# Retention heads in (batch, row) order: keys and values used as they were loaded

## The chip, the cores and the metric

The kernel runs on one core of one Trainium2 chip. The metric is the device time of one execution in microseconds, lower is better. Two figures appear below: the time of an execution, and the span of the profiled execution, from its first to its last instruction, which is a little shorter.

## The reference

Retention (attention with a decay instead of a softmax) on 8 batches, 8 heads, 576 positions and 64 dimensions, then a two-layer network with a hard-swish gate on the 4608 tokens of 512 values that come out.

```python
scores = scale * np.matmul(q, k.transpose(0, 1, 3, 2))
gamma = 1.0 - 2.0 ** (-5.0 - np.arange(H, dtype=np.float32))
rel = pos[:, None] - pos[None, :]
Dmat = np.where(rel >= 0, gamma[:, None, None] ** rel[None, :, :], 0.0)
attn = np.matmul(scores * Dmat[None, :, :, :], v)
x = np.ascontiguousarray(attn.transpose(0, 2, 1, 3)).reshape(B * S, H * D)
h = x @ w_in
out = (h * np.clip(h + 3.0, 0.0, 6.0) / 6.0) @ w_out
```

## The kernel before

**Blocks.** The 576 positions of a batch are cut into the first 64 (TL), here called the head block, and 512 more in four chunks of 128. Block 0 of the kernel (`kb` 0) holds the head blocks of all eight batches, 512 tokens; blocks 1 to 8 hold the other 512 positions of one batch each. In blocks 1 to 8 the positions before a chunk reach it through a running state per head, which begins with the state that the head block leaves. So block 0 has to give two things: its own outputs (`xts[0]`, the transposed input of the network), and for each batch and head a 64 by 64 state, the decayed product of keys and values (`zh`).

**Block 0 before the change.** Heads are taken in four pairs (`i` = 0 to 3, NP). `load_half` (line 415) and `load_values` (460) load one head of a pair for all batches: 128 partitions, each with four adjacent positions (`j`, NJ = 4) of 64 values, 1 KB. Position `4 r + j` of batch `b` lies in partition `8 r + b`. q and the first k are loaded in float32 by SP and ScalarE and cast by VectorE (`cast_heads`, 435); the other k and all v are loaded and cast to fp16 by DMAs that GpSimd issues. `turn_heads` (440) transposes k and q with TensorE; its moving operand `by_chunk` (84, 104) is a permuted identity that sorts the columns by batch, so that after the copy out of PSUM two batches stand side by side in each of four groups of 128 columns (`c`, NCB). `scores_heads` (492) then has one product of 128 by 128 for each group and head, and a masking product on VectorE with `hmask` (115, 152), 128 by 128 per head, which holds the decay and zero between the two batches of a group. The values are still in the order of the load: `values_heads` (470) sorts them with 32 products against `pick` (454, 456). The keys for the state are turned back by `keys_heads` (478) and scaled by their decay in `scaled_heads` (484). `inner_heads` (505) multiplies masked scores and sorted values, `head_states` (281) makes the states, `heads_decayed` (295) moves them to `zh`.

**After it.** `up_steps` (523) makes one unit of the up product of a block: four pairs of products (`product`, 154, two 64-column halves), a ScalarE pass (545) and a VectorE pass (547). Block 0 has 16 units; the first four are started in turn, interleaved. `fetch(8, wout[0])` (874) holds back SP's loads of the chunks until the first piece of w_out has landed. Later stages overlap the retention of block `kb + 1`, the up product of the next and the down product of the last block.

**Order.** The order on every engine is written out by hand (from line 794): each engine works through its instructions in program order, and a wait stops what is queued behind it. PSUM has two rings of buffers: `st` with two and `pp` with six, given out in turn, so a new tile waits until its buffer's last reader is done. GpSimd computes and also issues DMAs: first k and v, then four pieces of w_in (715), then four of w_out (723). DMAs of GpSimd share eight semaphores in turn, so a DMA is issued when the one eight places ahead has landed.

The diff touches these functions:

## Time and profile before

| what | value |
|---|---|
| median of 3 runs | 293.78 us (293.6 to 297.28) |
| profiled execution, its own time | 294.78 us |
| its span | 292.9 us |
| TensorE busy | 284.6 us, 97% |
| VectorE, ScalarE, GpSimd busy | 73%, 63%, 46% |
| granted TensorE clock | 1.00 |
| HBM read, written | 36.70 MB, 9.44 MB |

The profile names an instruction by the line of the kernel that wrote it and by its tiles, output first: `L502 ha<-hpa,ws` is line 502, writing `ha16` from the scores in PSUM and the mask, which lies in a tile of `ws`. PE is a product on TensorE, PEld its weight load, DVE is VectorE, ACT ScalarE, POOL GpSimd, SP the engine that issues most DMAs; a `q` behind the name means the engine's sequencer. Behind "idle before" stands how long the engine had waited and for whom. DMA queues: q1 is SP's, q10 ScalarE's, q0 GpSimd's. [...]

### The profile page before, as it was taken

Reading aid. Unit: us, or ns where it says so; the run is one execution under the profiler, and the core shown is the slowest. Engines: PE = TensorE matmul, PEld = TensorE weight load, DVE = VectorE, ACT = ScalarE, POOL = GpSimd, SP = SyncE. Lnnn points to the kernel's source line nnn. Section 1 sums busy time; section 2 is a strip of 40 time slices with the busy share of each in tenths; the row PEclk is TensorE's granted clock in tenths of the full one; section 3 lists DMA queues with packets and bytes.
Section 4 is the critical chain, followed back from the end, with each engine's and each line's share of the span. In section 5 each row is a group of like instructions: output and inputs, shape, how many; then the busy total and the mean of one; then the engine's idle time right before and its main releaser. Section 6 shows DMA issues by size and latency. Waiting matters only on the chain.

```text
span 292.9 us, 12624 instructions
## 1 busy us (share of the span) xinstructions
PE 284.6 (97%) x5574; PEld 222.4 (76%) x5574; DVE 214.8 (73%) x380; ACT 185.4 (63%) x326; POOL 133.8 (46%) x166
## 2 busy tenths in 40 slices
PE   7899999999999999999999999999999999999995
PEld 2776556887656589787778788878788977778894
DVE  7858948888866867789776978697868685747654
ACT  4968546856775877647675768476847574655420
POOL 8961148788651527066625662656265004000510
PEclk9999999999999999999999999999999999999999
DMA  7999999999999999979998999798916101200114
GB/s 161 166 204 214 238 233 219 244 226 226 208 167 199 187 238 197 190 202 215 281 183 202 174 235 143 191 180 221 124 69 102 51 4 65 83 0 2 74 74 143
DMA packets 119526, 47.86 MB, mean 163 GB/s; under 512 B 92336, under 2 KB 114864, under 8 KB 119472
## 3 DMA queue, kind: packets, MB, share of 16 engines
q1 hardware_dynamic: 114336, 41.56, 73.1%
q0 software_dynamic: 4704, 5.11, 10.7%
q8 instruction: 43, 0.70, 1.1%
q10 hardware_dynamic: 432, 0.39, 0.5%
q14 instruction: 11, 0.09, 0.1%
HBM read 36.70 MB, written 9.44 MB: 158 GB/s over the span
## 4 chain that ended last, share of the span: by engine, by line
PE 94%; DMA 2%; ACT 1%; issue 1%; DVE 0%; SPq 0%; DVEq 0%
PE ph L158 44%; PE pm L158 29%; PE pd L158 10%; PE po L241 4%; PE pa L241 2%; DMA hq<-in_q_dram 2%; PE pu L241 2%; PE hpv L158 1%; PE ptk L158 1%; PE ptq L158 1%; ACT hqT L449 1%; ACT hkT L451 0%; PE hpo L511 0%; PE hptq L444 0%; SPq L424 0%
## 5 line engine op out<-in xcount | busy, mean ns | idle before, releaser
L158 PE MATMUL ph<-xT,win 128*64 128x512 f16 (+1 forms) x1248 | 145.6, 364 | 0.3 <-issue 0.3
L547 DVE SCALAR_TENSOR_TENSOR g<-u,ph 128x512 f16<-128x512 f32 x132 | 89.6, 684 | 51.5 <-ACT u L545 51.2
L545 ACT ACTIVATE u<-ph,half 128x512 f32<-128x512 f32 x132 | 90.2, 690 | 42.4 <-PE ph L158 41.5
L158 PEld LDWEIGHTS <-win 128*64 128x64 f16 x1248 | 85.2, 136 | 26.1 <-issue 0.9
L158 PEld LDWEIGHTS <-g 128*64 128x64 f16 x928 | 53.3, 110 | 16.5 <-issue 0.7
L158 PEld LDWEIGHTS <-s 128*64 128x64 f16 x896 | 51.1, 110 | 8.1 <-issue 0.7
L158 PE MATMUL pm<-ws,s 128*64 128x256 f16 x672 | 46.1, 273 | 0.5 <-issue 0.5
L333 POOL TENSOR_TENSOR z<-z,gpow 128x256 f32<-128x256 f32 x24 | 15.5, 644 | 65.6 <-DVE z L332 47.7
L199 POOL TENSOR_TENSOR q<-fq,dec 128x512 f16<-128x512 f32 x31 | 35.7, 1171 | 8.5 <-DMA fq<-in_q_dram 8.5
L394 ACT CAST xT<-po 128x512 f16<-128x512 f32 (+1 forms) x36 | 21.8, 676 | 24.3 <-PE po L241 24.3
L651 POOL TENSOR_TENSOR u<-u,p 128x512 f32<-128x512 f32 x7 | 8.9, 1270 | 61.4 <-ACT u L692 55.2
L204 POOL TENSOR_TENSOR v<-fv,dec 128x512 f16<-128x512 f32 x32 | 35.6, 1113 | 0.1
L158 PE MATMUL pm<-wout,g 128*64 128x256 f16 x448 | 32.2, 273 | 0.0
L158 PE MATMUL pd<-wout,g 128*64 128x512 f16 x256 | 31.9, 380 | 0.3 <-issue 0.3
L276 DVE TENSOR_TENSOR a<-pa,mask 128x512 f16<-128x512 f32 (+1 forms) x36 | 21.0, 625 | 4.7 <-PE po L241 2.7
L587 DVE TENSOR_TENSOR s<-g 128x1024 f16<-128x1024 f16 x28 | 19.4, 695 | 0.2
L193 ACT CAST k<-fk 128x512 f16<-128x512 f32 x24 | 14.9, 621 | 4.0 <-DMA fk<-in_k_dram 4.0
L342 ACT CAST z<-z 128x512 f16<-128x512 f32 x24 | 14.9, 622 | 4.0 <-DVE z L329 4.0
L158 PE MATMUL pm<-ws,g 128*64 128x256 f16 x224 | 16.8, 274 | 0.0
L158 PE MATMUL pm<-wout,s 128*64 128x256 f16 x224 | 16.6, 273 | 0.0
L587 DVE TENSOR_TENSOR s<-g,s 128x1024 f16<-128x1024 f16 x14 | 12.1, 862 | 0.0
L241 PE MATMUL po<-qT,z 64*64 64x64 f16 x512 | 10.9, 196 | 0.3
(112 smaller groups left out, 280.8 us busy)
## 6 DMA issues: line engine op xcount, KB each, us to landing
fk<-in_k_dram SPq DMA_DIRECT2D x32, 256.0 KB, 4.6
fq<-in_q_dram SPq DMA_DIRECT2D x16, 512.0 KB, 5.9
fv<-in_v_dram SPq DMA_DIRECT2D x32, 256.0 KB, 5.8
out_dram<-o SPq DMA_DIRECT2D x14, 512.0 KB, 4.0
win<-in_moe_w_in_dram POOLq DMA_DIRECT2D x4, 512.0 KB, 9.0
wout<-in_moe_w_out_dram POOLq DMA_DIRECT2D x4, 512.0 KB, 17.1
out_dram<-o SPq DMA_DIRECT2D x7, 256.0 KB, 5.0
hq<-in_q_dram SPq DMA_DIRECT2D x6, 128.0 KB, 4.7
```

What stands on the lines that cost most here:

```text
L158: nc.tensor.matmul(out[r], lhs[:, r], rhs, skip_group_check=True, **flags)
L193: cast_keys = lambda: (nc.gpsimd.tensor_copy if c in K_POOL else nc.scalar.copy)(by_head(k16), in_rows(st[c]["fk"]))
L199: (nc.vector if e and c in Q_DVE else nc.gpsimd).tensor_tensor(by_head(q16[:, e]), in_rows(st[c]["fq"][:, :, e, :]), in_rows(dd[:, 2 + e, ...
L204: nc.gpsimd.tensor_tensor(v16, st[c]["fv"], dd[:, 1, H:2 * H, :], ALU.mult)
L241: return lambda: nc.tensor.matmul(*args, skip_group_check=True, **flags)
L276: nc.vector.tensor_tensor(a16[:, a, 0:n].rearrange("p x i q -> p (x i) q"), pa[a].rearrange("p x i q -> p (x i) q"), m, ALU.mult)
L333: nc.gpsimd.tensor_tensor(new, new, decay, ALU.mult)
L342: nc.scalar.copy(z16s[c], zs[c])
L394: nc.scalar.copy(xt[:, s], po[s].rearrange("p x n (e r) -> p x n e r", e=2))
L545: nc.scalar.activation(uu[:, 0:n], ph[:, 0:n], ACTF.Relu, bias=half, scale=1.0 / 6.0)
L547: nc.vector.scalar_tensor_tensor(out=g[:, hf, ths, jr, :], in0=by_half(uu), scalar=1.0, in1=by_half(ph), op0=ALU.min, op1=ALU.mult)
L587: nc.vector.tensor_tensor(*pend.popleft())
```

## The change

Loads put position `4 r + j` of batch `b` into partition `16 b + r`: the source is walked batch by batch instead of row by row. 32 partitions then hold two batches, and scores, inner and state products are made for each group of 32 partitions (`rows32`) and each `j`, with keys and values as they were loaded. q is still sorted by the copy that follows its turn. The score products grow from 8 to 32 for a pair of heads, the inner products from 8 to 32, the state products from 64 to 128 in all. The sorts (`values_heads`), the second turn of the keys (`keys_heads`, `scaled_heads`), `by_chunk`, `picks` and the clearing of `pick` go. The mask of a head has 134 columns instead of 128, and the four `j` read it at four shifted places. The decay of the keys moves to the values: `values_apart` writes, for each pair, the values of the even and of the odd batch of a group apart, with decay and zeros, on GpSimd for pairs 1 and 3 and on VectorE for 0 and 2. Inner products of all pairs gather in four PSUM tiles (`po`), copied out in eight pieces (`outputs_heads`). In the order, all masks and the exponents of k stand ahead of the turns of q, GpSimd's w_out DMAs stand behind its two `values_apart`, and 16 idle products stand ahead of the first up products. Cut to its core:

```diff
-        nc.gpsimd.iota(query, pattern=[[TL, 2], [1, NJ], [NJ, RP]], base=0, channel_multiplier=0,
+        nc.gpsimd.iota(query, pattern=[[P, 2], [1, NX]], base=1 - NJ, channel_multiplier=0,
                        allow_small_or_imprecise_dtypes=True)
...
-        nc.vector.tensor_copy(by_chunk.rearrange("p (c e r) -> p c e r", c=NCB, e=2),
-                              ident16.rearrange("p (r e c) -> p c e r", e=2, c=NCB))
...
+        if of == "k":
+            nc.vector.tensor_copy(fk[:, 0:1], fj[:, 0:1])
+            for e in range(2):
+                nc.vector.scalar_tensor_tensor(out=base[:, e:e + 1], in0=odd, scalar=(2 * e - 1) * FAR, in1=row,
+                                               op0=ALU.mult, op1=ALU.add)
+            nc.vector.tensor_scalar(base[:, 1:2], base[:, 1:2], 1.0, -FAR, ALU.mult, ALU.add)
+            nc.vector.tensor_tensor(fk[:, 1:].rearrange("p (e j) -> p e j", e=2), steps,
+                                    base.unsqueeze(2).to_broadcast([P, 2, NJ]), ALU.add)
...
-                nc.vector.tensor_scalar(arg[:, :, H + h], fj[:, 0:4], -lg, 0.0, ALU.mult, ALU.add)
+                nc.vector.tensor_scalar(argk[:, :, h], fk, -lg, 0.0, ALU.mult, ALU.add)
...
-    hmask = ws[3].rearrange("p j n -> p (j n)")[:, 0:H * P].rearrange("p (h q) -> p h q", h=H)
+    hmask = ws[3].rearrange("p j n -> p (j n)")[:, 0:H * 2 * NX].rearrange("p (h x) -> p h x", h=H)
...
-    def head_states(c0, tag):
...
+    def head_states(pu, i):
+        for j in range(NJ):
+            for t in range(NCB):
+                at = rows32(t)
                 for a in range(2):
-                    j, h2 = divmod(i + NP * a, 2)
-                    for e in range(2):
-                        todo[e].append(mm(pu[e][rows(a), c - c0, i], kn[rows(e), j, c, h2 * D:h2 * D + D],
-                                          vh[rows(e), c, j, h2, :], start=True, stop=True))
-        in_turn(todo)
-        return pu
-
-    def heads_decayed(c0, e, pu):
-        z, by = zh[:, c0 + NCB * e:c0 + NCB * e + 2], gpow.unsqueeze(1).unsqueeze(3).to_broadcast([P, 2, NP, D])
-        if e:
-            nc.scalar.copy(z, pu[e])
+                    n, h2 = divmod(i + NP * a, 2)
+                    nc.tensor.matmul(pu[t][rows(a), i], hd[n]["k"][at, h2, j, :], vh[n][at, h2, :, j, :],
+                                     start=(j == 0), stop=(j == NJ - 1), skip_group_check=True)
+
+    def heads_decayed(t, pu, on_dve):
+        z, by = zh[:, 2 * t:2 * t + 2], gpow.unsqueeze(1).unsqueeze(3).to_broadcast([P, 2, NP, D])
+        of = pu[t].rearrange("p i e d -> p e i d")
+        if on_dve:
+            nc.vector.tensor_tensor(z, of, by, ALU.mult)
+        else:
+            nc.scalar.copy(z, of)
             nc.gpsimd.tensor_tensor(z, z, by, ALU.mult)
...
-    def idle_products(n):
+    def idle_products(n, of=NP):
...
-    kn = ws[1].rearrange("p j n -> p (j n)").rearrange("p (i c x) -> p i c x", i=NP, c=NCB)
-    vh = ws[4].rearrange("p j n -> p (j n)").rearrange("p (c i e d) -> p c i e d", c=NCB, i=NP, e=2)
+    rows32 = lambda t: slice(2 * RP * t, 2 * RP * t + 2 * RP)
+    vh = [ws[1 + i // 2].rearrange("p j n -> p (j n)")[:, (i % 2) * 4 * NJ * D:(i % 2 + 1) * 4 * NJ * D].rearrange(
+        "p (h e j d) -> p h e j d", h=2, e=2, j=NJ) for i in range(NP)]
 
...
-                            dict(q=q, k=k, v=v)[nm][:, 2 * i + e, 0:TL, :].rearrange("b (r j) d -> r b (j d)", j=NJ))
+                            dict(q=q, k=k, v=v)[nm][:, 2 * i + e, 0:TL, :].rearrange("b (r j) d -> b r (j d)", j=NJ))
...
-                nc.tensor.matmul(pt[e * D:e * D + D, j, :], hd[i][nm][:, e, j, :], by_chunk, start=True, stop=True,
+                nc.tensor.matmul(pt[e * D:e * D + D, j, :], hd[i][nm][:, e, j, :], ident16, start=True, stop=True,
                                  skip_group_check=True)
...
+            t = half_tile(work, "qT", i, FP16, "hqT", bufs=3)
+            copy(t.rearrange("p (x r j) -> p x r j", j=NJ, r=RP), pt.rearrange("p j (x r) -> p x r j", r=RP))
+            hd[i]["qT"] = t.rearrange("p (t y) -> p t y", t=NCB)
...
-    def picks():
...
+            t = work.tile([P, H * D], FP16, tag="kT", bufs=4, name=f"hkT{i}").rearrange("p (j x) -> p j x", j=NJ)
+            copy(t, pt)
+            hd[i]["kT"] = t
...
-                                    v[:, 2 * i + e, 0:TL, :].rearrange("b (r j) d -> r b (j d)", j=NJ))
+                                    v[:, 2 * i + e, 0:TL, :].rearrange("b (r j) d -> b r (j d)", j=NJ))
...
-    def values_heads(i, copy):
...
-    def keys_heads(i, tag):
...
-    def scaled_heads(i, on_dve):
...
+    def values_apart(i, engine):
+        by = deck[:, 1:, 2 * i:2 * i + 2].rearrange("p (e j) h -> p h e j", e=2)
+        for h2 in range(2):
+            engine.tensor_tensor(vh[i][:, h2], hd[i]["v"][:, h2].unsqueeze(1).to_broadcast([P, 2, NJ, D]),
+                                 by[:, h2].unsqueeze(3).to_broadcast([P, 2, NJ, D]), ALU.mult)
 
     def scores_heads(i):
         kT, qT = hd[i]["kT"], hd[i]["qT"]
-        a16 = work.tile([P, 2, NCB, P], FP16, tag="a16", bufs=4, name=f"ha16_{i}")
-        pa = [psum.tile([P, NCB, P], FP32, tag="pp", name=f"hpa{h2}_{i}") for h2 in range(2)]
-        for c in range(NCB):
-            for h2 in range(2):
-                r = slice(h2 * D, h2 * D + D)
-                nc.tensor.matmul(pa[h2][:, c, :], kT[r, c, :], qT[r, c, :], start=True, stop=True)
+        a16 = work.tile([P, 2, NJ, P], FP16, tag="a16", bufs=4, name=f"ha16_{i}")
+        pa = [psum.tile([P, NJ, P], FP32, tag="pp", name=f"hpa{h2}_{i}") for h2 in range(2)]
+        for j in range(NJ):
+            for t in range(NCB):
+                for h2 in range(2):
+                    nc.tensor.matmul(pa[h2][rows32(t), NJ - 1 - j, :], kT[rows(h2), j, rows32(t)], qT[rows(h2), t, :],
+                                     start=True, stop=True, skip_group_check=True)
         for h2 in range(2):
-            m = hmask[:, 2 * i + h2:2 * i + h2 + 1, :].to_broadcast([P, NCB, P])
-            nc.vector.tensor_tensor(a16[:, h2], pa[h2], m, ALU.mult)
+            m = hmask[:, 2 * i + h2, :]
+            m = bass.AP(m.tensor, m.offset, [list(m.ap[0]), [1, NJ], [NX, 2], [1, TL]])
+            by_half = lambda t: t.rearrange("p j (e s) -> p j e s", e=2)
+            nc.vector.tensor_tensor(by_half(a16[:, h2]), by_half(pa[h2]), m, ALU.mult)
         hd[i]["a16"] = a16
 
-    def inner_heads(i, copy):
+    def inner_heads(i):
         if 0 not in xts:
             xts[0] = work.tile([P, NP, BLK], FP16, tag="xT", bufs=2, name="xT0")
-        po = psum.tile([P, NCB, P], FP32, tag="pp", name=f"hpo{i}")
-        for c in range(NCB):
-            for h2 in range(2):
-                nc.tensor.matmul(po[h2 * D:h2 * D + D, c, :], vh[:, c, i, h2, :], hd[i]["a16"][:, h2, c, :],
-                                 start=True, stop=True, skip_group_check=True)
-        copy(xts[0][:, i, :].rearrange("p (x r j) -> p x r j", r=RP, j=NJ),
-             po.rearrange("p c (e j r) -> p (c e) r j", e=2, j=NJ))
+            hd["po"] = [psum.tile([P, NP, P], FP32, tag="st" if t < 2 else "pp", name=f"hpo{t}",
+                                  **(dict(bufs=2) if t < 2 else {})) for t in range(NCB)]
+        for j in range(NJ):
+            for t in range(NCB):
+                at = rows32(t)
+                for h2 in range(2):
+                    nc.tensor.matmul(hd["po"][t][rows(h2), i, :], hd[i]["v"][at, h2, j, :], hd[i]["a16"][at, h2, NJ - 1 - j, :],
+                                     start=(j == 0), stop=(j == NJ - 1), skip_group_check=True)
+
+    by_pairs = lambda: xts[0].rearrange("p n x -> p (n x)").rearrange("p (g t i x) -> p g t i x", g=2, t=NCB, i=2)
+
+    def outputs_heads(g, t, copy):
+        copy(by_pairs()[:, g, t], hd["po"][t][:, 2 * g:2 * g + 2, :])
...
+        if kb == 0:
+            to, x = ph.rearrange("p (t x) -> p t x", t=NCB), lambda dmc: by_pairs()[:, dmc // 2, :, dmc % 2, :]
...
-                nc.gpsimd.memset(pick.rearrange("p j c m -> p (j c m)").bitcast(I32), 0)
+                nc.gpsimd.iota(steps, pattern=[[0, 2], [1, NJ]], base=0, channel_multiplier=0,
+                               allow_small_or_imprecise_dtypes=True)
         for i in range(NP):
             load_values(i)
         for n in range(4):
             win_piece(n)
-        wout = [wout_piece(pc) for pc in (0, 2, 1)]
-        decays_of_chunk()
-        wout.append(wout_piece(3))
-        decays("q")
-        mask_of_chunk()
         distances()
         idle_products(8)
-        mask_of_heads(0)
+        for i in range(3):
+            mask_of_heads(i)
         cast_heads(0, "k", on_dve)
-        picks()
         decays("k")
         turn_heads(0, "k", on_act)
-        mask_of_heads(1)
+        mask_of_heads(3)
+        exponents("k")
         idle_products(3)
         cast_heads(0, "q", on_dve)
-        mask_of_heads(2)
         turn_heads(0, "q", on_act)
         cast_heads(1, "q", on_dve)
         turn_heads(1, "k", on_act)
         turn_heads(1, "q", on_act)
         cast_heads(2, "q", on_dve)
         scores_heads(0)
-        mask_of_heads(3)
-        exponents("k")
-        keys_heads(0, "pp")
         turn_heads(2, "k", on_act)
         turn_heads(2, "q", on_act)
         cast_heads(3, "q", on_dve)
         scores_heads(1)
-        keys_heads(1, "pp")
         turn_heads(3, "k", on_act)
         turn_heads(3, "q", on_act)
         scores_heads(2)
-        scaled_heads(0, False)
-        values_heads(0, on_act)
+        inner_heads(0)
         scores_heads(3)
-        scaled_heads(1, False)
-        values_heads(1, on_act)
-        inner_heads(0, on_act)
-        values_heads(2, on_dve)
-        inner_heads(1, on_dve)
-        values_heads(3, on_act)
-        inner_heads(2, on_dve)
-        keys_heads(2, "st")
-        scaled_heads(2, True)
+        inner_heads(1)
+        for t in range(NCB):
+            outputs_heads(0, t, on_act)
+        for i in (1, 3):
+            values_apart(i, nc.gpsimd)
+        wout = [wout_piece(pc) for pc in (0, 2, 1)]
+        decays_of_chunk()
+        wout.append(wout_piece(3))
+        decays("q")
+        mask_of_chunk()
+        inner_heads(2)
+        values_apart(0, nc.vector)
+        inner_heads(3)
+        idle_products(16, 1)
+        for t in range(NCB):
+            outputs_heads(1, t, on_act if t % 2 else on_dve)
+        values_apart(2, nc.vector)
         first = [up_steps(0, u) for u in range(4)]
-        for unit in first:
-            next(unit)
-        inner_heads(3, on_act)
-        keys_heads(3, "st")
-        scaled_heads(3, False)
-        for unit in first:
-            next(unit)
+        for _ in range(2):
+            for unit in first:
+                next(unit)
         for unit in first:
             for _ in unit:
                 pass
-        heads = [head_states(0, "pp"), head_states(2, "st")]
+        pu = [psum.tile([P, NP, 2, D], FP32, tag="st" if t < 2 else "pp", name=f"hpu{t}",
+                        **(dict(bufs=2) if t < 2 else {})) for t in range(NCB)]
+        for i in range(NP):
+            head_states(pu, i)
         fetch(8, wout[0])
-        heads_decayed(0, 0, heads[0])
         for u in range(4, NFC):
             up_unit(0, u)
             if u == 4:
-                heads_decayed(0, 1, heads[0])
+                heads_decayed(2, pu, True)
+            elif u == 5:
+                heads_decayed(3, pu, False)
             elif u == 9:
-                heads_decayed(2, 0, heads[1])
+                heads_decayed(0, pu, True)
             elif u == 10:
-                heads_decayed(2, 1, heads[1])
+                heads_decayed(1, pu, False)
             elif u == 12:
                 exponents("q")
         weight_sums(3, 1, 2, 4)
```

## The prediction

> **What bounds the kernel now.** I read the page first. TensorE is busy for nearly all of the span, so the change can only matter where TensorE isn't yet full, or by what it makes TensorE wait for later.

> ```profile
> PE 284.6 (97%) x5574; PEld 222.4 (76%) x5574; DVE 214.8 (73%) x380; ACT 185.4 (63%) x326; POOL 133.8 (46%) x166
> ```

> So I went to the chain in order of time for the start of the span. Its columns are start, length, and what the chain runs through.

> ```profile
> 1.57 5.63 DMA hq<-in_q_dram
> ...
> 16.18 0.89 PE hpv L158 x32
> 17.08 0.22 PE hpo L511 x8
> 17.30 0.22 PE hpk L158 x8
> ...
> 21.66 0.67 PE pu L241 x64
> 22.33 10.51 PE ph L158 x96
> ```

> From 22.33 on TensorE runs up products without a gap (96 in 10.51 us, 0.1095 us each), and what follows is untouched. The change is worth what it does to that one time stamp, plus any later wait that it makes. Before it lie the q load, the turns, and, until 17.1, the sorting of values on TensorE (`hpv`). The timeline of VectorE shows what runs beside that.

> ```profile
> 9.83 1.29 DVE L502 TENSOR_TENSOR ha<-hpa,ws 128x512 f16<-128x512 f32 x2 [0.47 <-PE hpa L499]
> 11.04 0.42 DVE L437 CAST hq<-hq 128x512 f16<-128x512 f32 x1
> 11.37 3.85 DVE L502 TENSOR_TENSOR ha<-hpa,ws 128x512 f16<-128x512 f32 x6
> ```

> VectorE masks scores until 15.22 with no gap after the last cast of q (0.64 us a mask): the masks follow that cast by queue order, and the cast needs the last q load. The third view is the DMA of the first 14.2 us.

> ```profile
> DMA  0000004899869899999999999999999999897936
> ...
> q0 software_dynamic: 2078, 0.98, 59.2%
> q1 hardware_dynamic: 1008, 0.92, 23.0%
> q10 hardware_dynamic: 432, 0.39, 10.3%
> ```

> After six empty slices (2.1 us) the engines are full: 92.5% of 14.2 us of sixteen engines. The packets also tell how a load is spread: q10 carries three loads of 128 rows, 384 packets, and has 432; q1 seven loads, 896, and has 1008. Each load brings 16 short packets more. Every load of today has a source whose outermost loop counts 16 (`r b (j d)`) or a multiple of it.

> **Part one, what is taken off TensorE.** The four value sorts are 128 products of 0.0278 us (0.89 us for 32), 3.6 us on the chain; the four key turns 4 x 0.22 = 0.9 us. The sorting copies behind them go from ScalarE and VectorE, such as

> ```profile
> L476 ACT CAST ws<-hpv 128x512 f16<-128x512 f32 x3 | 1.8, 585 | 1.2 <-PE hpv L158 1.2
> ```

> Of these 4.5 us little comes back: the masks end at 15.22 either way, and the last inner product, the up products and the states stand behind them.

> **Part two, what is added before the up products.** The masks keep their size (six after the cast, 3.85 us). Behind them VectorE now has two products of `values_apart(0)`, 512 elements each, then two of the four copies of `outputs_heads(1, t)`, 256 elements out of PSUM. The first is nearest to a half of q16 on VectorE, the second to a state sum:

> ```profile
> L199 DVE TENSOR_TENSOR q<-fq,dec 128x512 f16<-128x512 f32 x1 | 0.7, 693 | 1.7 <-DMA fq<-in_q_dram 1.7
> ...
> L329 DVE TENSOR_TENSOR z<-pa,zh 128x256 f32<-128x256 f32 x1 | 0.4, 425 | 0.6 <-PE pa L241 0.6
> ```

> That is 1.38 + 0.85 us. The copies make a new wait: the four first up units take PSUM buffers in turn, and the second and third take those of `po` 2 and 3, so only the first product pairs of unit 0 can run before both copies of `po` 2 are done. Everything on TensorE queues behind that wait, and ScalarE and VectorE wait for its `ph`. ScalarE's share of the copies ends earlier, since it has only waited for the same inner product.

> After it come 32 up products less one pair, 3.50 - 0.22 = 3.28 us, then the states: 128 products of 32 rows and 128 columns instead of 64 of 64 and 64. 32-row tiles stand nowhere in the trace. Today's 64 take 0.67 us, 10.5 ns each; two at a time, as in the sort, would take 13.9, so more than two run at once. Low end: eight at a time, 128 x 27.8 / 4 = 0.89 us. High end: two at a time, 3.56 us. I take the rate of the nearest row, 10.5 ns, 1.34 us. Scores and inner products (32 for 8 per pair of heads, each) cost 0.34 us for 0.22 by it, beside the masks, which take 1.28 us a pair; without that cover they would add 0.1 us a pair.

> If the loads land as now, the cast starts at 11.04 and the sum is 11.04 + 0.42 + 3.85 + 1.38 + 0.85 + 0.1 (handovers) + 3.28 + 1.34 = 22.26: nothing gained (22.33).

> The rest of the front is covered.

> ```profile
> L118 ACT ACTIVATE ws<-early,scale 128x128 f16<-128x128 f32 x8 | 2.7, 394 | 1.3 <-DVE early L113 1.3
> ```

> These masks of ScalarE now all stand ahead of the q turns, with the exponents of k, from 4.9 to 8.2, where ScalarE waits for q (the cast of q came at 7.3); uncovered they would add 0.7 us. `decays("k")` gains five tiny steps where VectorE waits for q as well. Up products read `xT` in pieces of 128 columns, still 512 a product. GpSimd gets four products of 512 elements at 1.11 us, 4.5 us ahead of the four w_out DMAs, the powers, `decays("q")` and the chunk mask. Behind w_out wait SP's loads:

> ```profile
> L199 POOL TENSOR_TENSOR q<-fq,dec 128x512 f16<-128x512 f32 x6 | 6.6, 1113 | 8.5 <-DMA fq<-in_q_dram 8.5
> ```

> ```profile
> 14.55 1.64 POOL L724 DMA_DIRECT2D wout<-in_moe_w_out_dram x3
> ```

> ```profile
> SPq L179 <- DMA wout<-in_moe_w_out_dram: 22.3, 1, 22.3
> ```

> ```profile
> L719 POOL DMA_DIRECT2D win<-in_moe_w_in_dram x4: 760/765/797, 11.6 to 13.8; - x4
> ...
> DMA to landing us min/median/max: 5.9/9.0/12.6
> ```

> The last w_in piece, issued at 13.8, lands 12.6 us later, at 26.4. The DMA engines limit that stream, so w_out issued at 19 instead of 14.6 still finds w_in in front of it: covered as long as it is issued before some 26.

> **Part three, the loads.** All 24 head loads keep their bytes and 128 rows of 1 KB, but the source now reads `b r (j d)`: the outermost loop counts 8. What this costs isn't in the trace. Bounds: nothing, if the rows are dealt out as before; and twice the engines' time for these loads, if a load is shared out along that loop, as the 16 closing packets beside an outer 16 suggest, so that eight engines carry it. I take the second, as the nearest reading of the packets.

> [...]

> The price, from rows. The last q load is issued at 5.8 and lands some 4.7 us on, at 10.5:

> ```profile
> L424 SPq DMA_DIRECT2D hq<-in_q_dram x6: 536/599/797, 1.6 to 5.8; - x6
> ...
> DMA to landing us min/median/max: 4.3/4.7/5.6
> ```

> Hardware loads (q1 and q10) are 33.3% of 14.2 us, 4.73 us on each of sixteen engines; software head loads 59.2%, less some first w_in packets, 8.2 us. Between 2 and 11 us the engines work off 110%, 1.10 us per us:

> ```profile
> q0 software_dynamic: 1413, 0.65, 57.9%
> q1 hardware_dynamic: 1008, 0.92, 36.3%
> q10 hardware_dynamic: 432, 0.39, 16.2%
> ```

> With 8 of the 14 software loads (4.7 us) served beside them, the last q load would land at 2.1 + (4.73 + 4.7) / 1.10 = 10.7: the model holds for today. On eight engines the hardware part is 9.46 us. With 8 of 14 software loads beside it: 2.1 + 14.2 / 1.10 = 15.0; with all of them: 2.1 + 17.7 / 1.10 = 18.2. I take 15.8, near the low end, since the last software loads are issued late. The cast then starts at 15.8 instead of 11.04, with masks of three pairs still behind it, and the up products run free at 22.26 + 4.76 = 27.0, that is 4.7 us later than now. The weights are delayed by about as much (the eight engines hold 17.7 us of head loads instead of 12.9), so SP's loads stay in step with TensorE.

> **The sum.** The profiled execution took 294.78 us for its span of 292.9, which is 1.0 above the median of 293.78.

> ```profile
> span 292.9 us, 12624 instructions
> ```

> 294.78 + 4.7 = 299.5 on its scale; on that of the median 298.5.

> **The rivals.** First, not slower: the loads land as now, because rows are dealt out over sixteen engines whatever the outer loop. For it: nothing in the trace shows a load on fewer. Against: the closing packets. The sum above then gives 22.26, or 293.7 us; with states at either end 293.2 to 295.9. It decides if the last q load lands by 11.0.

> Second, TensorE works at half rate, or its 32-row products take turns. The first idle products show a half rate:

> ```profile
> 1.85 3.63 PE L158 MATMUL idle<-ident 128*64 128x512 f16 x16 [1.85 <-POOL ident masks.py:199]
> ```

> 0.227 us each against 0.1095. With q late, TensorE has little to do from 7.2 to some 20. Up products of units 0 to 3 at half rate cost 3.3 us more, states two at a time 2.2: 300.7 to 301.8 with late loads. Against: the sixteen idle products put ahead of them, and gaps of one or two us only.

> [...]

> Third, w_out comes too late. With v landing at 18, GpSimd would issue w_out near 21. If w_in has run dry by then, the loads of chunk 4 slip; now q16 starts only just before its turn:

> ```profile
> 39.34 1.46 POOL L199 TENSOR_TENSOR q<-fq,dec 128x512 f16<-128x512 f32 x1 [8.49 <-DMA fq<-in_q_dram]
> ...
> 41.31 0.66 PEld L158 LDWEIGHTS <-q 128*64 128x64 f16 x16
> ```

> That leaves 0.5 us; 3 us of slip beyond TensorE's own would give 301. Against: w_in would then end near 30.

> **How the numbers follow.** Forecast 0.60 (298.5; 297 to 301 by its bounds), not slower 0.22 (293.7), half rate or serial products 0.13 (301), w_out 0.05 (301). The 2% that a measurement of this kernel can tell from no change is 5.9 us: 299.7 and 287.9. Slower by that: a quarter of the forecast's case (0.16), nearly all of the second rival (0.12), most of the third (0.04): 0.32. Faster by that: no case reaches it, 0.02 for what I don't see; within it 0.66. The range takes in the rival of the other side and the upper bounds: 293.0 to 302.0.

> **What would show it.** Right: hq's landings stretch from 4.7 to 8 us and more, the last cast of q on VectorE starts near 15.8, q10 has 408 packets for its three loads (8 closing ones each), and the run of 96 up products starts near 27, with masks, two products and two copies back to back ahead of it on VectorE. Wrong: the cast at 11 with 432 packets (first rival); states over 2 us, or up products of units 0 to 3 at 0.2 us each (second); TensorE's `ptq` later behind the 96 up products than now (third).

## The result and the profile after

The changed kernel is slower: 304.33 us (median of 4 runs, 302.35 to 305.37) against 294.2 for the kernel before beside it, a ratio of 1.0314 with an interval of 1.0222 to 1.0406. The profiled execution took 304.93 us for a span of 303.1. The forecast of 298.5 and its range up to 302.0 lie below.

The chain in order of time (start, length, what it runs through) again gives the time stamp that the prediction is about:

```profile
6.76 7.78 DMA hk<-in_k_dram
...
18.61 1.88 PE hpo L502 x50
20.50 0.67 PE idle L167 x9
21.17 1.25 issue
22.42 1.49 PE idle L167 x23
23.91 5.25 PE ph L167 x32
29.15 1.22 PE hpu L296 x128
30.38 10.51 PE ph L167 x96
```

The 96 up products start at 30.38 instead of 22.33, 8.05 us late, and themselves take 10.51 us as before. The remaining 2.1 us or so of the span are lost later. Three things in these rows have no counterpart before: a pause in which TensorE waits for nothing that the profile shows ("issue"), 32 up products at 0.164 us each (5.25 us over 32) where 0.1095 were forecast, and, behind the pause, idle products that were to fill a gap and now come after it. Such rates are the length of a group over its count, since the products overlap: the page has 0.367 us as the mean of one product of `ph`, and 146.3 us as busy time of all 1248. VectorE's timeline has the fourth:

```profile
14.44 0.43 DVE L443 CAST hq<-hq 128x512 f16<-128x512 f32 x1 [0.72 <-DMA hq<-in_q_dram]
...
18.93 4.65 DVE L474 TENSOR_TENSOR ws<-hv,deck 128x512 f16<-128x512 f16 x2
23.50 0.74 DVE L508 CAST xT<-hpo 128x256 f16<-128x256 f32 x2
24.17 1.28 DVE L474 TENSOR_TENSOR ws<-hv,deck 128x512 f16<-128x512 f16 x2
```

The two products of `values_apart(0)` take 4.65 us; the same two for pair 2 take 1.28 at 24.17. What differs is GpSimd, which makes its own four products of line 474 in the same time (4.6 us by the groups of instructions).

The windows view gives the granted clock (the number behind POOL's):

```profile
10.00:15.00 5.00, 3.80 (x100) 2.60 (x99) 2.61 (x6) 2.35 (x5) 2.61 (x5) 0.53 1.10 161
15.00:20.00 5.00, 4.56 (x195) 3.09 (x193) 4.63 (x7) 2.27 (x6) 5.00 (x7) 0.50 0.89 117
...
26.00:28.00 2.00, 2.00 (x15) 1.35 (x13) 0.00 (x0) 0.10 (x1) 1.68 (x10) 0.65 1.26 214
```

TensorE runs at half clock from soon after 10 us to 27.4 (0.65 over the last window is a half for 1.4 of its 2 us), though it counts as busy for 4.56 of the 5 us from 15 to 20, with the new small products. The kernel before has 1.00 from 7.58 us to its end. The stretch just ahead of the drop shows TensorE waiting for the casts of late q loads, busy for 1.09 of 3.41 us:

```profile
6.93:10.34 3.41, 1.09 (x18) 0.55 (x16) 0.63 (x2) 1.13 (x4) 2.76 (x5) 1.00 1.07 200
```

The pause is read from windows that all begin at zero: the numbers behind the first two busy times are TensorE's products and weight loads so far.

```profile
0.00:22.00 22.00, 15.59 (x351) 9.04 (x351) 13.64 (x43) 10.27 (x25) 16.57 (x31) 0.74 0.85 141
0.00:90.00 90.00, 82.14 (x1757) 56.17 (x1758) 67.71 (x133) 52.29 (x101) 58.46 (x94) 0.91 1.05 195
...
0.00:156.00 156.00, 146.44 (x3035) 106.00 (x3036) 116.89 (x212) 96.61 (x177) 88.93 (x123) 0.95 1.07 199
```

Each window ends inside a pause (from 21.17, 89.24 and 155.54). The sums are 702, 3515 and 6071 instructions: 11 and 21 times 256 above the first, within 7 (some records can be missing). Counted the same way, every pause of TensorE over 0.12 us behind its first 20 instructions that has no releaser, in all fourteen traces of this case, stands within some 15 of such a multiple. So in these traces TensorE makes such stops only where a block of 256 instructions ends. The queue that carries instructions (q8) fits:

```profile
q0 software_dynamic: 6496, 5.12, 10.8%
q8 instruction: 44, 0.72, 1.0%
q10 hardware_dynamic: 408, 0.39, 0.4%
```

44 packets of 16 KB for 11,404 products and weight loads (2 x 5702), one for every 259. The first packet behind a block's edge at 17.0 starts at 20.16, and TensorE goes on 2.26 us after that. The kernel before has the same edge, ahead of its states, at 21.65, and does not stop there: its packet started at 18.17. In both kernels the packet starts about 3 us after TensorE passed the block's edge ahead of it (17.0 here, 15.35 before) and takes 0.9; the difference is how soon the block at hand is used up, in 4.2 us here and in 6.3 before. What starts a packet, no trace shows. Single pauses of this kind last up to 3.79 us in the runs here (`before_split_sort`, 16.87 to 20.66).

### The profile page after: what moved, and what is told of

Read it like the earlier page. It is cut to its first block, busy times and chain, and to the rows that moved or that the text cites. A ratio compares the mean times of both kernels' runs of the same rounds, so it can differ in the third digit from the quotient of the medians.

```text
span 303.1 us, 12880 instructions
## 1 busy us (share of the span) xinstructions
PE 288.8 (95%) x5702; PEld 223.5 (74%) x5702; DVE 219.4 (72%) x381; ACT 182.2 (60%) x321; POOL 139.6 (46%) x170
## 3 DMA queue, kind: packets, MB, share of 16 engines
q0 software_dynamic: 6496, 5.12, 10.8%
## 4 chain that ended last, share of the span: by engine, by line
PE 92%; DMA 4%; issue 2%; POOL 1%; DVE 0%; ACT 0%
PE ph L167 42%; PE pm L167 29%; PE pd L167 9%; DMA hk<-in_k_dram 4%; PE po L250 4%; PE pa L250 2%; PE pu L250 2%; PE hpo L502 1%; PE ptk L167 1%; PE idle L167 1%; PE ptq L167 1%; POOL hk L430 1%; PE hpu L296 0%; PE hpa L484 0%; PE hptk L450 0%
## 5 line engine op out<-in xcount | busy, mean ns | idle before, releaser
L167 PE MATMUL ph<-xT,win 128*64 128x512 f16 (+1 forms) x1248 | 146.3, 367 | 0.0
L167 PEld LDWEIGHTS <-s 128*64 128x64 f16 x896 | 50.4, 110 | 8.7 <-issue 1.1
L208 POOL TENSOR_TENSOR q<-fq,decq 128x512 f16<-128x512 f32 x31 | 35.8, 1176 | 5.4 <-DMA fq<-in_q_dram 5.4
L213 POOL TENSOR_TENSOR v<-fv,deck 128x512 f16<-128x512 f32 x32 | 36.5, 1142 | 0.0
L167 PE MATMUL pm<-wout,g 128*64 128x256 f16 x448 | 31.5, 273 | 0.0
L583 DVE TENSOR_TENSOR s<-s,g 128x1024 f16<-128x1024 f16 x14 | 11.2, 799 | 0.0
```

The source lines that it names most:

```text
L167: nc.tensor.matmul(out[r], lhs[:, r], rhs, skip_group_check=True, **flags)
L208: (nc.vector if e and c in Q_DVE else nc.gpsimd).tensor_tensor(by_head(q16[:, e]), in_rows(st[c]["fq"][:, :, e, :]), in_rows(by_row(decq[: ...
L213: nc.gpsimd.tensor_tensor(v16, st[c]["fv"], by_row(deck[:, 0]), ALU.mult)
L583: nc.vector.tensor_tensor(*pend.popleft())
```

## The experiments

**One half of the change at a time.** `after_rows_first` is the changed kernel with the old load order, `before_batch_first` the kernel before with the new one, in both load functions:

```diff
-  ...rearrange("b (r j) d -> b r (j d)", j=NJ)
+  ...rearrange("b (r j) d -> r b (j d)", j=NJ)
```

> The changed kernel with the head loads walked row by row as in the kernel before (outermost loop 16 instead of 8); values then lie in other partitions than the products take them from, so the output is not the reference's; instructions and sizes are those of the changed kernel. If the late loads are the cause of most of the loss: q10 has 432 packets again, the last cast of q starts at 11 instead of 14.4, the granted clock stays at 1.00 through the front, and the run of 96 up products starts near 24 to 25 (30.4 in the changed kernel): 297 to 299 us. If the loads matter little and the new work on VectorE and TensorE is the cause: the cast comes earlier but the 96 start at 28 or later, 302 us or more.

> The kernel before with nothing changed but the walk of the head loads (batch by batch, outermost loop 8); the output is not the reference's, as values lie in other partitions. Late loads alone as the cause: q10 has 408 packets, the last cast of q starts near 14.4 instead of 11.0, the 96 up products start near 25.7 if the clock holds (297 us) and 28 to 29 if it drops to half as in the changed kernel (300 us). If the loads aren't the cause: 294 us.

The new loads alone cost less than forecast: ratio 1.0086 (1.005 to 1.0123), the 96 at 25.74, 3.4 us late, of which 2.2 are left at the end of the span (295.1). They also take the clock to half, from 10.18 to 17.01, but it is back before the up products. All the rest alone costs nearly everything: ratio 1.0272 (1.0239 to 1.0306), the 96 at 28.44, although the last q is cast at 10.93, as before the change. VectorE's timeline in `after_rows_first`, and then its chain:

```profile
10.93 0.42 DVE L443 CAST hq<-hq 128x512 f16<-128x512 f32 x1
...
15.55 4.05 DVE L474 TENSOR_TENSOR ws<-hv,deck 128x512 f16<-128x512 f16 x2
19.52 0.74 DVE L508 CAST xT<-hpo 128x256 f16<-128x256 f32 x2
```

```profile
17.60 2.85 issue
20.44 1.49 PE idle L167 x13
21.93 5.28 PE ph L167 x32
```

With loads in time, the prediction's sum gave 22.26. The run has the same parts and 6.2 us more. A pause of 2.85 us and VectorE's slow pair end within 0.2 us of each other (20.44 and 20.26), so each could hide the gain from removing the other. That was tried.

**VectorE's slow pair.** `after_copies_first` puts `values_apart(0)` behind the copies that the up products wait for; `after_apart_on_dve` takes GpSimd's products away from beside it:

```diff
 inner_heads(2)
-values_apart(0, nc.vector)
 ...
     outputs_heads(1, t, on_act if t % 2 else on_dve)
+values_apart(0, nc.vector)
 values_apart(2, nc.vector)
```

```diff
-for i in (1, 3):
-    values_apart(i, nc.gpsimd)
 ...
 values_apart(2, nc.vector)
+for i in (1, 3):
+    values_apart(i, nc.vector)
```

> The changed kernel with the two products of values_apart(0) on VectorE put behind the copies of outputs_heads(1, t) instead of ahead of them; nothing else. Theory: they stand on the path and take 4.65 us there, since GpSimd works on its own values_apart at the same time. Then the copies end near 19.8 instead of 24.2; the up products of units 0 to 3 still run at half rate, so the 96 start 2 to 3.5 us earlier: 301 us. Rival: half the clock alone sets the start of the 96; then less than 1 us is gained.

> The changed kernel with values_apart of pairs 1 and 3 on VectorE behind pair 2 instead of on GpSimd, so that GpSimd does nothing beside values_apart(0), which stays ahead of the copies. If the 4.65 us of its two products come from GpSimd working beside them, each takes 0.7 us here, 1.4 in all, and the 96 start about 2 us earlier or more. If the form of the product itself is slow (fp16 input spread over two places), they stay at 2.3 us each, and six of them now take 14 us, which delays the states: slower than the changed kernel.

Neither is faster: ratios 1.0283 (1.0222 to 1.0343) and 1.0308 (1.0266 to 1.0351). A row of VectorE's timeline in `after_apart_on_dve`, and one of the chain of `after_copies_first`:

```profile
19.37 1.28 DVE L474 TENSOR_TENSOR ws<-hv,deck 128x512 f16<-128x512 f16 x2
```

```profile
20.78 2.48 issue
```

With GpSimd silent the pair takes 1.28 us, so GpSimd's products beside it cost 3.4. By what means they slow it is not shown. But where the copies end early (20.9 in `after_copies_first`, 22.1 in `after_apart_on_dve`), the pause holds TensorE until 23.26 and 23.55. Taking away one of two waits that end together gained nothing.

**Instructions alone.** `before_split_sort` is the kernel before with each sorting product split into two of 64 columns: 256 instructions more, no small tiles, old loads, no products on GpSimd. (Its sorted values aren't the reference's.) `before_rows_early` has 256 more as well, but as idle products in the first 7 us.

```diff
-product(pv[:, c], pick[:, j, c, :], hd[i]["v"][:, :, j, :], ...)
+for e in range(2):
+    product(pv[:, c, e], pick[:, j, c, :], hd[i]["v"][:, e, j, :], ...)
```

```diff
-idle_products(8)
+idle_products(72, 1)
+idle_products(3)
 ...
-idle_products(3)
```

> The kernel before with each sorting product of the values split into two of 64 columns: the same array work and the same loads, 256 rows more in TensorE's program, all of them in the sort. Theory of supply: a pause of 2 us or more without a releaser at row 449 or 705, and the 96 up products start at 24.5 to 27 instead of 22.3: 297 to 299 us. Rival: rows cost nothing by themselves; the 96 start at 22.3 to 23 and the time is that of the kernel before.

> The kernel before with 256 TensorE rows more, all of them idle products of 128 columns in the first 7 us, where TensorE waits for loads (72 narrow ones and 3 wide ones in place of 11 wide ones); all else as before, and the edges of the row blocks fall on the same instructions as before, one block later. Theory (a pause needs a block that is used up before the next one has come; rows that are issued early cost nothing): the 96 up products start at 22.3 to 23, no pause over 0.6 us, 294.5 to 296.5 us against 295.5 for before, ratio 0.998 to 1.004. Rival (each row more costs in all, as the 256 rows of the split sorting did with 6.5 us): 301 to 303. A third: the narrow products lower the clock, then the front is 1 to 2 us late, 297 to 298.

Splitting the sort alone brings nearly two thirds of the loss, more than the theory of the expectation had: ratio 1.0196 (1.0148 to 1.0244), 302.71 us, the 96 at 28.42. Its chain, and two windows, one that ends at its first pause and one in its second:

```profile
16.87 3.79 issue
20.66 1.07 PE hpv L158 x55
...
22.21 1.71 PE ph L158 x8
...
28.42 0.58 PE ph L158 x4
```

```profile
0.00:14.20 14.20, 10.43 (x223) 6.67 (x223) 11.02 (x41) 9.88 (x23) 12.82 (x27) 1.00 0.94 165
0.00:19.00 19.00, 12.86 (x351) 8.97 (x351) 13.19 (x44) 11.48 (x26) 17.20 (x49) 1.00 1.01 174
```

The 256 instructions between the two edges (446 and 702) are worked off from 14.46 to 16.87, 2.4 us; the next block is there 6.2 us after the edge. After the long pause the clock is at half (0.50 from 22 to 24), and eight up products take 1.71 us. The same number put early costs a fifth of that: ratio 1.0044 (1.0014 to 1.0074), 297.15 us, no pause over 0.4 us. Its front is 2.2 us late, near the third case of the expectation: the narrow products last until 7.95, in the way of the k turns, and the clock is at 0.54 from 12 to 15. So what cost here was not so much the instruction as a block that was used up before the next one was in.

**Clock and block.** `after_rows_wide` is `after_rows_first` with two groups of three wide idle products (six halves each) among the small ones; `after_one_win` loads and uses one piece of w_in instead of four; `after_no_idle` drops the 16 idle products ahead of the up products, 64 instructions:

```diff
 scores_heads(2)
+idle_products(3)
 inner_heads(0)
 scores_heads(3)
+idle_products(3)
```

```diff
-for n in range(4):
-    win_piece(n)
+win_piece(0)
```

```diff
-idle_products(16, 1)
```

> The changed kernel with the loads walked row by row (the output is not the reference's) and two groups of six wide idle products (128 rows, 64 by 512) put among its small products, ahead of inner_heads(0) and of inner_heads(1). Theory: runs of 32-row and 32-column products don't count as work for TensorE's clock, which is why it fell to half at 15 us in the run with the loads alone changed although TensorE was busy. Then the clock stays at 1.00, units 0 to 3 take 3.5 us instead of 5.3, and the 96 start about 1 us earlier than there (28.4), with the pause of instructions unchanged. Rival: the clock falls because of the pauses; it still falls at 15 to 18 us.

> The changed kernel with only the first of the four w_in pieces loaded and used for all up products (the output is not the reference's), so that the DMA engines have little to do between 18 and 23 us. Theory of supply: the next block of TensorE's program comes within 3.5 us instead of 5.5 to 6.6, the pause of 1.25 us ahead of the idle products goes, and the 96 start 1 to 2 us earlier. Rival: the pause has nothing to do with the DMA load; it stays at 1 to 3 us.

> The changed kernel without the 16 idle products ahead of the first up products, 64 rows of TensorE's program fewer. Theory of supply: TensorE's program comes in blocks of 256 rows (every pause without a releaser in these traces stands at row 193 plus a multiple of 256), a block is asked for when the one ahead of it is entered, and beside the weight stream it takes 5.5 to 6.6 us; rows of small products are eaten faster. The pause then stays until about 22.4 us but lies among the first up products, and the 96 start about 1.5 us earlier than 30.4: 302.5 us. Theory that the idle products keep the clock up: units 0 to 3 take longer than 5.3 us and nothing is gained.

First `after_rows_first`, then `after_rows_wide`, by windows:

```profile
15.00:17.60 2.60, 2.53 (x73) 1.67 (x72) 2.60 (x3) 1.46 (x5) 2.60 (x4) 0.55 1.21 198
```

```profile
15.00:17.20 2.20, 1.62 (x93) 1.04 (x87) 2.20 (x3) 1.20 (x4) 2.20 (x4) 1.00 1.22 192
17.20:20.00 2.80, 0.09 (x11) 0.00 (x0) 2.80 (x2) 0.37 (x1) 2.80 (x3) 0.81 1.24 206
20.00:24.00 4.00, 3.99 (x45) 2.73 (x46) 2.00 (x5) 0.37 (x1) 3.64 (x21) 0.50 1.24 207
```

With the six wide products the clock stays at 1.00 past 17.2. In a pause of 2.72 us behind them it falls all the same, to 0.50 by 20.0, and the first up products take 5.28 us again. Ratio 1.0238 (1.0186 to 1.0289). That small products don't count, the theory of the expectation, does not follow, and other runs contradict it. In these traces the clock changes only at points that lie 3.41 us, or a multiple of it, apart (10.24, 17.07, 20.48 and 27.31 in `after_copies_no_idle`). In the step ahead of the drop at 15.26, from 11.85, `after_rows_first` has TensorE busy for 2.06 of 3.41 us; in the step from 12.09 to 15.50 `after_rows_wide` has 3.22, its wide products among them. Small products that filled a step did as well. First two steps of `after_copies_no_idle`, then two of `after_rows_copies_no_idle` (both below), which has no wide products among its small ones either:

```profile
13.65:17.07 3.42, 3.41 (x143) 2.39 (x142) 3.05 (x6) 1.07 (x2) 3.42 (x6) 0.50 0.95 94
17.07:20.48 3.41, 1.43 (x64) 0.88 (x63) 2.22 (x5) 1.85 (x6) 3.41 (x4) 1.00 1.18 193
```

```profile
10.99:14.40 3.41, 2.48 (x144) 1.62 (x144) 3.08 (x7) 1.46 (x3) 3.25 (x5) 1.00 1.00 111
14.40:17.82 3.42, 1.76 (x90) 1.08 (x68) 2.43 (x5) 1.85 (x6) 3.42 (x5) 1.00 1.23 199
```

The first of these steps has 128 small products (scores and inner products) and the last 11 turns, and the clock is back behind it; the third has nearly the same products, and it stays. So in these runs the drops go with waits, not with the size of products. How much waiting a step may hold is not shown: `before_split_sort` kept its clock behind a step with 1.68 us busy (15.19 to 18.60).

With a single piece of w_in the pause stays, 1.38 us (20.29 to 21.66), and the 96 start at 29.63, 0.75 us earlier. That does not clear the weight stream: the loads that were left kept the DMA engines full until 19.2 (share 1.16 from 16.0 to 19.2, 0.07 from there to 20.3), and the packet of the late block started at 19.16, just as they ran dry. Whether it waited for them stays open. Ratio 1.0226 (1.0176 to 1.0276).

Without the idle products the block's edge falls behind the first up products and the pause ahead of them is gone; in its place the chain has a load:

```profile
6.34 6.60 DMA hk<-in_k_dram
...
13.22 1.28 POOL hv L465 x2
14.50 5.79 DMA win<-in_moe_w_in_dram
...
20.33 6.40 PE ph L167 x16
```

The late k holds GpSimd's next issue, and so the first piece of w_in, until 20.29. The 96 start at 28.50, 1.9 earlier, and the profiled execution, 303.11 us, keeps that gain; the other executions don't (ratio 1.0281, 1.0208 to 1.0354), and no profile shows where they lose it.

**All at once.** Both kernels have `values_apart(0)` behind the copies and no idle products; the first has the old load order too:

> The changed kernel with three of its edits taken out of the front: loads in (row, batch) order (so the output is not the reference's: the masks and the state products expect the other order), the 16 idle products gone (64 TensorE rows fewer before the up products), and values_apart(0) behind the copies of the outputs. Theory (the front is a sum of parts that hide one another: late loads, the pause at the edge of TensorE's row block, half clock, the two engines' products): with all but the half clock gone, the last q cast ends at 10.9, the state outputs at 16.9, row 705 falls inside the first up products, and the 96 up products start at 24 to 26 (22.3 before, 28.4 with the loads alone turned back); 299 to 301 us. Rival (each 32-row product costs for itself, wherever it stands): the 96 start at 27 or later, as with the loads alone, 302 to 304.

> The changed kernel with its own (batch, row) loads, values_apart(0) behind the copies of the outputs and the 16 idle products gone; the output stays the reference's. Theory: the copies end near 20.9 as when they were first put ahead, row 705 now stands 18 rows into the up products instead of at their head, and the first w_in piece lands near 20; the first up products start at 20.5 to 21 and run at half clock, the 96 start at 27.5 to 28.5 (30.4 in the changed kernel); 301.5 to 303. Rival (the pause moves with the row, its length stays): the 96 start at 30 or later, 304.

The first has its 96 at 26.43, above the 24 to 26 of the expectation, since a further edge (958 instructions in) falls into the state products and costs 1.59 us; its time of 302.45 us lies among those of the rival, by pauses further on; ratio 1.0228 (1.0181 to 1.0276). The second, with the new loads, waits for w_in until 22.0; 96 at 29.47, ratio 1.032 (1.0272 to 1.0368), above its expectation. The start of the 96 and what the span has behind it, by kernel:

| kernel | 96 start | span less start | ratio |
|---|---|---|---|
| before | 22.33 | 270.6 | 1 |
| before_masks_early (below) | 22.42 | 270.8 | 1.001 |
| before_rows_early | 24.57 | 269.5 | 1.0044 |
| before_batch_first | 25.74 | 269.4 | 1.0086 |
| after_rows_copies_no_idle | 26.43 | 274.2 | 1.0228 |
| before_split_sort | 28.42 | 272.6 | 1.0196 |
| after_rows_first | 28.44 | 273.7 | 1.0272 |
| after_no_idle | 28.50 | 272.8 | 1.0281 |
| after_rows_wide | 28.68 | 271.4 | 1.0238 |
| after_copies_no_idle | 29.47 | 275.7 | 1.032 |
| after_one_win | 29.63 | 271.8 | 1.0226 |
| after | 30.38 | 272.7 | 1.0314 |
| after_copies_first | 31.12 | 272.1 | 1.0283 |
| after_apart_on_dve | 31.16 | 272.0 | 1.0308 |

The third column is one execution each. It falls for the two kernels that start 2 to 3.5 us late and rises by 0.8 to 5.1 us for all that start 4 us late or more. In the trace of the changed kernel that rise is pauses at block edges:

```profile
PE po L250 <- issue: 1.3, 1, 1.3
PE idle L167 <- issue: 1.2, 1, 1.2
PE pm L167 <- issue: 1.2, 3, 0.6
PE pd L167 <- issue: 1.1, 1, 1.1
```

These are TensorE's waits without a releaser in the changed kernel. Without the one in the front (`idle`) they sum up to 3.6 us; the kernel before has 0.5, 0.3, 0.3 and 0.3, so the difference is about the 2.1 of the span. The late edges of the changed kernel, such as those at 3515 and 6071, lie on the same instructions as edges of the kernel before and of `before_rows_early` (whole blocks were added); at these two, where it loses 1.13 and 1.29 us, the kernel before loses 0.25 and 0.31 and `before_rows_early` no more than 0.12. Why a late start makes the stops longer stays open.

**A try at a faster kernel.** The kernel before, with ScalarE's masks and exponents ahead of the q turns as in the change:

```diff
-mask_of_heads(0)
+for i in range(3):
+    mask_of_heads(i)
 ...
-mask_of_heads(1)
+mask_of_heads(3)
+exponents("k")
```

> The kernel before with the masks of pairs 1 to 3 and the exponents of the keys' decays on ScalarE ahead of its copies of turned queries, instead of between them (one mask of 0.59 us and the exponents of 0.12 us leave the chain to the last q cast). Theory (the chain of the first q copies sets the front by 0.5 us of slack at the row blocks): the 96 up products start 0.3 to 0.7 us earlier, ratio 0.997 to 1.000. Rival (the masks now delay the first copy of turned keys, which is the chain): 0 to 1 us later, ratio 1.000 to 1.004.

No difference: ratio 1.001 (0.9987 to 1.0032). Its chain no longer has the q load; it has GpSimd's loads and, in passing, the edge of a block:

```profile
11.64 5.65 DMA win<-in_moe_w_in_dram
...
17.34 1.08 PE ph L158 x8
...
21.64 0.10 issue
...
22.42 10.51 PE ph L158 x96
```

So, by the chains of these two traces, the front before is held by three things that end close together: the q chain, the first piece of w_in, and a block of TensorE's program. No version tried beats it.

## Why the prediction was wrong

**The forecast named the loads and put the rest at nothing; the rest cost more than the loads.** "If the loads land as now ... 22.26: nothing gained" is the step that failed: measured, with those loads, 28.44. The 6.2 us between are a product pair that was priced too low, a pause for instructions and half clock, in what follows.

**The loads: right in kind, oversized.** q10 has 408 packets, 8 closing ones each, and the median landing of the k loads went from 4.7 to 6.8 us (6.2 to 7.8). No view shows over how many engines a load was spread: the eight of the sum were the author's estimate from the closing packets. The last q cast starts at 14.44, not 15.8. Alone the loads cost 3.4 us at the 96, half clock until 17.01 included; on top of the rest they cost 1.9 (28.44 to 30.38). What the prediction missed is that software loads also grew: q0 has 6496 packets for 4704, 128 more for each of 14 loads. And the chain of the changed kernel goes through k, by way of GpSimd's queue, not through q; the last k and the last q come close together, and in `after_copies_first` it is q.

**`values_apart(0)`, mis-sized.** 1.38 was taken from a lone product on VectorE, 4.65 measured. GpSimd's products were in the plan at the same moment ("4.5 us ahead of the four w_out DMAs") and were checked only for what they delay on GpSimd.

**The instructions of the small products, left out.** They were priced by rate on TensorE: states 1.34, measured 1.22, so the rate of 32-row tiles was right (9.5 ns). That 256 instructions more (11,404 for 11,148) must be brought in has no term. The sort and key turns that were removed are fewer and longer products; what replaced them uses up a block in 4.2 us (17.0 to 21.17) where the next one takes 5.4 to come.

**Half clock, in the wrong place.** It stood as a rival at 0.13 with 3.3 us; it came, for 2.0 us (5.25 for 3.28, the clock being back at 27.41), and came together with the forecast instead of in its place. Its reason agrees with the trace: with q late TensorE was busy for 1.09 of the 3.41 us ahead of the drop. The argument against it fell: the drop at 10.34 lies behind a wait of 2.01 us (to 9.15) and in one of 0.55 us (to 10.62), "gaps of one or two us only", and the idle products came 10 us behind the drop, with a block's edge among them.

**By the sum, for the changed kernel itself:** 27.0, less 1.36 for the earlier cast, plus 0.3 for masks that waited, 3.3 for `values_apart(0)`, 2.0 for the clock, less 0.8 for copies, handovers and states that were a little shorter, gives 30.4 (30.38 measured). The 0.8 is what the other terms leave. The pause of 1.25 with the idle products behind it ends at 23.91, beside VectorE's copies (24.24), and so does not add here; it holds the front as soon as VectorE is relieved. To that come some 2 us of later pauses, which had no term either.

**The other rivals.** Not slower did not happen: the condition, q landed by 11.0, failed. Where it held, in `after_rows_first` with its last cast at 10.93, the time was 303.63 us, not 293.7. Chunk loads behind w_out, the third, were in time: TensorE's waits name no such load.

## What to carry to other kernels

Count TensorE's instructions, not only its time: where a dense stretch uses up 256 products and weight loads faster than a block came here (5.4 to 6.7 us), look for "issue" pauses at equal distances in the count, and rather keep fewer, longer products. Before taking a wait off the chain, list what ends within a microsecond of it; here pairs of such waits (a slow VectorE pair and a late block, a late block and a late weight piece) hid each other's repair. And price a VectorE product of two SBUF operands with GpSimd's products beside it, not alone (4.65 us against 1.28 here).
